# Banded attention and a gated feed-forward block on one core: loads issued as two or four transfers of shorter rows

## The chip, the cores and the metric

The kernel runs on one core of a Trainium2 chip. The metric is the device time of one execution in microseconds (us), taken as the median of several runs. TensorE is called PE here, VectorE DVE, ScalarE ACT, and SyncE SP; SP issues nearly all transfers between the chip's main memory and the on-chip buffer.

## The reference

For 8 batches, 8 heads, 576 positions and 64 numbers per head, queries and keys give scores, and only a band of them is kept: the last 32 positions in heads 0 to 3, every fourth of the last 128 positions in heads 4 to 7. After a softmax the scores weigh the values. The heads of a batch stand side by side as `x`, and a block with a three-tap convolution and a gate follows:

```python
scores = scale * np.matmul(q, k.transpose(0, 1, 3, 2))
scores = np.where(masks[None, :, :, :], scores, -1000000000.0)
...
attn = attn / (np.sum(attn, axis=-1, keepdims=True) + 1e-09)
return np.matmul(attn, v).astype(np.float32)
...
h = np.maximum(x @ w_in, 0.0)            # 512 -> 1024
conv_out += conv_w[k][None, None, :] * hp[:, k:k + S, :]
gate = 1.0 / (1.0 + np.exp(-conv_out))
return (h * gate @ w_out).astype(np.float32)
```

`w_in`, `conv_w` and `w_out` arrive as 64-bit floats, so a weight takes 8 bytes in main memory.

## The kernel before

Attention works on pairs of heads: 8 batches by 4 pairs make 32 units. A unit loads its queries and keys as one tile `qk` of 128 partitions by 1184 numbers (592 KB, rows of 4736 bytes) and its values as one tile `v` of 128 by 768 numbers (384 KB, rows of 3072 bytes). One unit (batch 0, pair 1, by the constant `SPLIT`) has its `qk` load cut in two by columns already, of 608 and 576 numbers, so that PE can begin on the first. There are two `qk` buffers and three `v` buffers; a load into a buffer waits until PE has read what stood there. PE makes the scores in a burst of 72 small matmuls (L281), DVE and ACT make the softmax (L306 to L331), DVE transposes the result (L333), PE multiplies with the values in a burst of 80 or 84 small matmuls (L349), and the result is stored as a high part and a low part, `x…a` and `x…b`.

The feed-forward block of a batch multiplies `x` with `w_in` (L408, results in `mm` or `nn`), makes the convolution and the gate on ACT and DVE (L414 to L432), and multiplies with `w_out` (L448); ACT scales the result (L457) and SP stores it (L463). Each weight is held as a high and a low part too. The function `weights` makes these: it loads a chunk of 1 MB (128 rows of 8192 bytes) into one of two buffers `raw` (L507), and five DVE operations and one ACT copy turn it into the two parts (L513 to L522). There are four such chunks for `w_in` and four for `w_out`.

No loop sets the order of the program. Each piece of work is a task of a planner; the table `TURNS_OF` gives each task its turn, and the tasks are issued in order of their turns. Every engine works through its own instructions in that order. A task that loads a tile is one turn; the table has one entry for each, and its entries are the same before and after the change.

Transfers report through semaphores. The kernel's framework has eight of them for the transfers of SP and ACT (DMAHW0 to DMAHW7 in the rows below) and gives them out in turn, one to each transfer. A transfer that gets a semaphore whose earlier transfer has not landed waits for that landing.

Of the kernel before, what the change touches and what calls it, by code (L numbers as in the profile page):

```python
# [37 lines left out]
I32 = mybir.dt.int32  # L38
# [169 lines left out]
def attn_moe(ctx: ExitStack, tc: tile.TileContext, qk_p, qk_d, v_p, v_d, w_in, w_out, conv, mask, out):  # L208
    nc = tc.nc
# [10 lines left out]
    few = [const.tile([128, 3 * NF], F32, name=f"few{i}") for i in range(2)]  # L220
    plan = Planner()

    def slots(name, n, shape, dtype=F32, parts=1, pool=const):
        make = lambda i: [pool.tile(shape, dtype, name=f"{name}{i}{'abc'[j] if parts > 1 else ''}") for j in range(parts)]
        made = [make(i) for i in range(n)]
        plan.pool(name, made if parts > 1 else [m[0] for m in made])
        return made

    slots("qk", 2, [128, QK])
    slots("v", 3, [128, NV, 128])  # L230
    ss = slots("s", 3, [128, 9, W + 1])
    slots("m", 3, [128, 9])
    slots("z", 3, [128, 9])
# [21 lines left out]
    def attention(b, p):  # L255
        kind = p // 2
        qk, v, s, m, z, pt, x = (Buffer(n) for n in ("qk", "v", "s", "m", "z", "pt", "x"))
# [3 lines left out]
        masked_by_pe = MASKED >> bit & 1  # L261
        xs[b, p] = x
        cuts = (0, S // 2 + 320, QK) if SPLIT >> bit & 1 else (0, QK)
        lqs = [plan.add(lambda lo=lo, hi=hi: nc.sync.dma_start(
            out=qk.t[:, lo:hi], in_=(qk_p, qk_d)[kind][b, p % 2][:, lo:hi]), uses=[qk])
            for i, (lo, hi) in enumerate(zip(cuts, cuts[1:]))]
        lv = plan.add(lambda: nc.sync.dma_start(
            out=v.t, in_=(v_p, v_d)[kind][b, p % 2]), uses=[v])

        block = lambda i: sc[i >= CUT].t[:, W * (i - CUT * (i >= CUT)):][:, 0:W] if early else sc[0].t[:, SC0 + W * i:SC0 + W * i + W]  # L270
        ranges = ((0, CUT), (CUT, 9)) if early else ((0, 9),)
# [2 lines left out]
        def scores(columns, final):  # L274


            for i in range(CUT):
                for c, j, hd, quad, s0, n in TURNS:
                    if i < n and c in columns:
                        q0, k0 = 32 * (s0 + i) + (S // 2 + 608) * c, S // 2 + 32 * (HALVES * c + s0 + i)  # L280
                        nc.tensor.matmul(block(s0 + i)[quad * 32:quad * 32 + 32], qk.t[hd * 64:hd * 64 + 64, q0:q0 + 32],  # L281
                                         qk.t[hd * 64:hd * 64 + 64, k0:k0 + W],
                                         start=not masked_by_pe or (quad, j) not in begun, stop=True,
                                         skip_group_check=True)
                        begun.add((quad, j))
            if masked_by_pe and final:
                for a, z in ((0, CUT), (CUT, 9)):
                    o = sc[a > 0].t[:, 0:W * (z - a)] if early else sc[0].t[:, SC0 + W * a:SC0 + W * z]
                    nc.tensor.matmul(o, ident16, mask_sb[:, kind, W * a:W * z], start=False, stop=True, skip_group_check=True)

        last = None
        for i, lq in enumerate(lqs):
            final = i == len(lqs) - 1
            last = plan.add(lambda cols=(i,) if len(lqs) > 1 else (0, 1), final=final: scores(
                cols, final), [last, lq], [qk, *sc, s])
# [8 lines left out]
        if not masked_by_pe:  # L304
            for a, e in ranges:
                last = plan.add(lambda a=a, e=e: nc.vector.tensor_tensor(  # L306
                    out=s.t[:, a:e, 0:W], in0=span(a, e), in1=masked[:, a:e], op=ALU.add), [last], [*sc, s])
        for a, e in ranges if masked_by_pe else ((0, 9),):
            last = plan.add(lambda a=a, e=e: nc.vector.tensor_reduce(  # L309
                out=m.t[:, a:e], in_=given(a, e), axis=AX.X, op=ALU.max, negate=slotwise), [last], [s, m, *held])  # L310
        if slotwise:
            last = plan.add(lambda: nc.scalar.mul(out=m.t, in_=m.t, mul=SCALE), [last], [m])
# [6 lines left out]
            last = plan.add(exps, [last], [s, m, z, *held])  # L319
            last = plan.add(lambda: nc.scalar.add(out=z.t, in_=z.t, add=1e-9), [last], [z])  # L320
        else:
            for a, e in ranges if masked_by_pe else ((0, 9),):
                last = plan.add(lambda a=a, e=e: nc.vector.tensor_tensor(
                    out=s.t[:, a:e, 0:W], in0=given(a, e), in1=wide(m.t, a, e), op=ALU.subtract), [last], [s, m, *held])
            last = plan.add(lambda: nc.scalar.activation(
                out=flat(), in_=flat(), func=AF.Exp, scale=SCALE), [last], [s])

            last = plan.add(lambda: nc.vector.tensor_reduce(  # L328
                out=z.t, in_=s.t, axis=AX.X, op=ALU.add), [last], [s, z])
        last = plan.add(lambda: nc.vector.reciprocal(out=z.t, in_=z.t), [last], [z])  # L330
        last = plan.add(lambda: nc.vector.tensor_tensor(  # L331
            out=flat(), in0=flat(), in1=wide(z.t), op=ALU.mult), [last], [s, z])
        last = plan.add(lambda: nc.vector.transpose(  # L333
            out=pt.t.rearrange("p (a k) -> p a k", k=W), in_=flat()), [last], [s, pt])
# [20 lines left out]
        last = plan.add(values, [lv, last], [v, pt, tv, x])  # L355

        def made(t):
            whole = tv.t.rearrange("p (c m) -> p c m", c=2)[:, :, TV0:TV0 + 2 * RUN]
            if kind == 0:
                return t.rearrange("p (c m) -> p c m", c=2), whole  # L360
            return t.rearrange("p (m c r) -> p m c r", c=2, r=2), whole.rearrange("p c (r m) -> p m c r", r=2)
# [10 lines left out]
        last = plan.add(lambda: nc.scalar.copy(out=made(x.t[0])[0], in_=made(x.t[0])[1]), [last], [tv, x])  # L372
        if HELPED >> (b * NP + p) & 1:
            def less():
# [3 lines left out]
            last = plan.add(less, [last], [tv, x])  # L378
            return [plan.add(lambda: nc.scalar.copy(
                out=made(x.t[1])[0], in_=made(x.t[1])[1]), [last], [tv, x])]  # L380
# [114 lines left out]
    def weights(src, hi, lo):  # L495

        raw, tb = Buffer("raw"), Buffer("t")
        n = src.shape[1]
        rate = n / PAIRED
        part = lambda i: raw.t[:, 0:2 * n].rearrange("p (n w) -> p n w", w=2)[:, :, i]  # L500
        lw, hw = (lambda i=i: part(i) for i in range(2))
        t = lambda: tb.t[:, 0:n]
        bits = lambda: tb.t.bitcast(I32)[:, 0:n]
        shaped = lambda x, like: x.rearrange("p (a c) -> p a c", a=like.shape[1])
        whole = lambda x: x.rearrange("p a b c -> p a (b c)") if len(x.shape) == 4 else x
        hi, lo = whole(hi), whole(lo)
        load = plan.add(lambda: nc.sync.dma_start(  # L507
            out=raw.t[:, 0:2 * n], in_=src.bitcast(I32)), uses=[raw])

        def step(after, run, uses=(raw, tb)):  # L510
            return plan.add(run, after, uses)

        last = step([load], lambda: nc.vector.tensor_scalar(  # L513
            out=t(), in0=hw().bitcast(F32), scalar1=2.0 ** -112, scalar2=None, op0=ALU.mult))
        last = step([last], lambda: nc.vector.tensor_scalar(  # L515
            out=bits(), in0=bits(), scalar1=3, scalar2=None, op0=ALU.logical_shift_left))
        last = step([last], lambda: nc.vector.scalar_tensor_tensor(  # L517
            out=bits(), in0=hw(), scalar=-0x80000000, in1=bits(), op0=ALU.bitwise_and, op1=ALU.bitwise_or))
        last = step([last], lambda: nc.vector.scalar_tensor_tensor(  # L519
            out=bits(), in0=lw(), scalar=29, in1=bits(), op0=ALU.logical_shift_right, op1=ALU.bitwise_or))  # L520
        high = plan.add(lambda: nc.scalar.copy(out=hi, in_=shaped(t(), hi)), [last], [tb])
        return [high, step([high], lambda: nc.vector.tensor_tensor(  # L522
            out=lo, in0=shaped(t(), lo), in1=hi.bitcast(F32), op=ALU.subtract), [tb])]
# [18 lines left out]
    for h, in hs:  # L542
        nc.gpsimd.memset(h[:, 0:1], 0.0)
        nc.gpsimd.memset(h[:, S + 1:S + 2], 0.0)
    converted = lambda src, pair: weights(src, *pair)
    wired = [converted(w_in[c], (wi[0][c], wi[1][c])) for c in range(4)]
    conved = few_weights(conv)
    wored = [converted(w_out[c], [wo[j][c % 2][:, :, c // 2] for j in range(2)]) for c in range(4)]
    ready = [[attention(b, p) for p in range(NP)] for b in range(B)]
    for b in range(B):  # L550
        expert(b, ready[b], wired, wored, conved)
# [68 lines left out]
```

## Time and profile before

| | |
|---|---|
| median of 3 runs | 511.15 us |
| lowest and highest of them | 510.21 and 513.08 us |
| the profiled execution, its own time | 514.47 us |
| span of the profiled execution, first to last instruction | 512.8 us |
| PE busy with matmuls | 494.7 us, 96% of the span |
| DVE, ACT busy | 370.3 us, 262.2 us |
| bytes moved | 50.95 MB, 99 GB/s over the span |

The span is what the rows of the profile divide up; the time of the execution is 1.67 us longer. The profiled execution is one single execution, 3.3 us above the median of the runs. Idle time of an engine matters only where another engine, or the end, waits for it.

### The profile page before, as it was taken

The page shows a single profiled execution, that of the slowest core. Times are in us where ns is not written, and L with a number is a line of the kernel's source. Part 1 is how long each engine was busy: PE and PEld are TensorE (multiplying, and loading weights), DVE is VectorE, ACT ScalarE, POOL GpSimd, SP SyncE. Part 2 cuts the span into 40 slices and gives each one's busy share as a digit, 9 for nine tenths or more (in the row PEclk, how much of TensorE's full clock was granted, in tenths as well). Part 3 has the DMA queues.
Part 4 walks back from the last instruction along what each step waited for, and adds up shares of the span by engine and source line. Part 5 has one row for each costly group of instructions (what it writes and reads, how often), then busy time and mean ns, then how long its engine had stood idle before and what let it go on. Part 6 is the DMA issues. An engine that isn't in the chain of part 4 may idle for free.

```text
span 512.8 us, 16447 instructions
## 1 busy us (share of the span) xinstructions
PE 494.7 (96%) x7466; PEld 441.0 (86%) x7466; DVE 370.3 (72%) x543; ACT 262.2 (51%) x559; POOL 1.4 (0%) x27
## 2 busy tenths in 40 slices
PE   4797999999999999999999999999999999999997
PEld 2686999999988898888898888889888988999885
DVE  3987999999999888976797558776686227644710
ACT  3547787554654356452664445535464426534611
POOL 1000000000000000000000000000000000000000
PEclk9999899999999999999999999999999999999999
DMA  8957337032432434423133122411120100001111
GB/s 302 366 190 266 111 117 282 1 100 65 140 114 89 146 100 119 141 78 115 32 121 128 62 80 64 129 58 57 32 75 1 42 20 22 22 1 41 42 41 61
DMA packets 16692, 50.95 MB, mean 99 GB/s; under 512 B 2032, under 2 KB 3184, under 8 KB 15600
## 3 DMA queue, kind: packets, MB, share of 16 engines
q1 hardware_dynamic: 16480, 49.84, 29.0%
q8 instruction: 58, 0.95, 0.8%
q10 hardware_dynamic: 144, 0.08, 0.1%
q14 instruction: 10, 0.08, 0.0%
HBM read 40.48 MB, written 9.44 MB: 97 GB/s over the span
## 4 chain that ended last, share of the span: by engine, by line
PE 94%; DVE 3%; DMA 1%; issue 1%; SPq 0%; ACT 0%; ACTq 0%
PE nn L448 40%; PE mm L408 39%; PE att L349 6%; PE att L281 5%; PE nn L408 3%; DMA qk<-in_qk_p_dram 1%; PE att L376 1%; DVE t L517 0%; DVE t L519 0%; DVE m L309 0%; DVE s L331 0%; DVE pt L333 0%; DVE z L328 0%; DVE t L515 0%; DVE t L513 0%
## 5 line engine op out<-in xcount | busy, mean ns | idle before, releaser
L448 PE MATMUL nn<-wo,g 128*128 128x512 f32 (+1 forms) x960 | 227.4, 373 | 0.0
L448 PEld LDWEIGHTS nn<-wo,g 128*128 128x128 f32 x960 | 160.4, 188 | 23.0
L418 DVE SCALAR_TENSOR_TENSOR c<-h,conv_sb,c 128x576 f32<-128x576 f32 x128 | 102.3, 810 | 33.0 <-ACT c L423 32.0
L414 ACT ACTIVATE h<-mm 128x288 f32<-128x288 f32 x120 | 48.6, 409 | 93.5 <-PE mm L408 93.3
L432 DVE TENSOR_TENSOR g<-c,g 128x576 fp32r<-128x576 f32 x64 | 47.8, 751 | 32.9 <-ACT g L431 32.5
L429 DVE SCALAR_TENSOR_TENSOR c<-c,h 128x576 f32<-128x576 f32 x64 | 47.6, 751 | 14.2 <-ACT c L427 13.9
L431 ACT CAST g<-c 128x576 fp32r<-128x576 f32 x64 | 42.5, 671 | 29.4 <-PE nn L448 14.9
L423 ACT ACTIVATE c<-h,conv_sb 128x576 f32<-128x576 f32 x64 | 49.2, 775 | 15.6 <-DVE g L432 15.0
L427 ACT ACTIVATE c<-c 128x576 f32<-128x576 f32 x64 | 42.9, 682 | 20.2 <-DVE c L418 20.0
L457 ACT ACTIVATE out<-nn 128x512 f32<-128x512 f32 (+1 forms) x40 | 21.9, 552 | 47.9 <-PE nn L448 41.8
L408 PE MATMUL mm<-x4a,wi 128*128 128x288 f32 x160 | 45.2, 301 | 0.0
L349 PEld LDWEIGHTS att<-pt,v 32*64 32x64 f32 x2624 | 33.7, 142 | 9.5 <-issue 5.9
L408 PE MATMUL mm<-x2a,wi 128*128 128x288 f32 x144 | 41.2, 301 | 0.0
L408 PE MATMUL mm<-x3a,wi 128*128 128x288 f32 x144 | 40.8, 302 | 0.0
L408 PE MATMUL mm<-x0a,wi 128*128 128x288 f32 x144 | 40.7, 300 | 0.0
L349 PE MATMUL att<-pt,v 32*64 32x64 f32 (+1 forms) x2624 | 37.4, 243 | 2.1 <-DVE pt L333 1.2
L408 PE MATMUL mm<-x6a,wi 128*128 128x288 f32 x128 | 35.7, 300 | 0.0
L408 PE MATMUL mm<-x5a,wi 128*128 128x288 f32 x128 | 35.7, 296 | 0.0
L281 PEld LDWEIGHTS att<-qk 64*32 64x32 f32 x2088 | 23.8, 106 | 11.7 <-issue 7.9
L281 PE MATMUL att<-qk 64*32 64x64 f32 x2088 | 29.0, 227 | 4.9 <-issue 3.2
L408 PE MATMUL mm<-x1a,wi 128*128 128x288 f32 x112 | 32.0, 303 | 0.0
L408 PEld LDWEIGHTS mm<-x4a,wi 128*128 128x128 f32 x160 | 29.8, 188 | 1.5 <-ACT h L414 0.2
(129 smaller groups left out, 748.3 us busy)
## 6 DMA issues: line engine op xcount, KB each, us to landing
qk<-in_qk_d_dram SPq DMA_DIRECT2D x16, 592.0 KB, 4.6
qk<-in_qk_p_dram SPq DMA_DIRECT2D x15, 592.0 KB, 4.3
out_dram<-out SPq DMA_DIRECT2D x28, 256.0 KB, 2.1
v<-in_v_p_dram SPq DMA_DIRECT2D x16, 384.0 KB, 4.4
v<-in_v_d_dram SPq DMA_DIRECT2D x16, 384.0 KB, 3.8
raw<-in_w_in_dram SPq DMA_DIRECT2D x4, 1024.0 KB, 7.0
raw<-in_w_out_dram SPq DMA_DIRECT2D x4, 1024.0 KB, 7.3
out_dram<-out SPq DMA_DIRECT2D x16, 128.0 KB, 2.4
```

The costliest lines, as they stand in the source:

```text
L281: nc.tensor.matmul(block(s0 + i)[quad * 32:quad * 32 + 32], qk.t[hd * 64:hd * 64 + 64, q0:q0 + 32], qk.t[hd * 64:hd * 64 + 64, k0:k0 + W], ...
L349: nc.tensor.matmul(tv.t[hd * 64:hd * 64 + 64, o:o + hi - lo], v.t[quad * 32:quad * 32 + 32, i, hd * 64:hd * 64 + 64], pt.t[quad * 32:quad ...
L408: nc.tensor.matmul(ps.t[:, 0:HALF], wi[jw][fc // 2][:, fc % 2, k], x[k].t[jx][:, hf * HALF:hf * HALF + HALF], start=(k == 0 and i == 0), s ...
L414: relu.append(plan.add(lambda fc=fc, hf=hf, ps=ps: nc.scalar.activation(out=h[fc].t[:, 1 + hf * HALF:1 + hf * HALF + HALF], in_=ps.t[:, 0: ...
L418: nc.vector.scalar_tensor_tensor(out=c[fc].t, in0=h[fc].t[:, k:S + k], scalar=conv_sb[:, k, fc:fc + 1], in1=c[fc].t, op0=ALU.mult, op1=ALU ...
L423: t = plan.add(lambda fc=fc: nc.scalar.activation(out=c[fc].t, in_=h[fc].t[:, 1:S + 1], func=AF.Copy, scale=conv_sb[:, 1, fc:fc + 1]), [re ...
L427: t = plan.add(lambda fc=fc: nc.scalar.activation(out=c[fc].t, in_=c[fc].t, func=AF.Tanh, scale=0.5), [t], [c[fc]])
L429: t = plan.add(lambda fc=fc: nc.vector.scalar_tensor_tensor(out=c[fc].t, in0=c[fc].t, scalar=1.0, in1=h[fc].t[:, 1:S + 1], op0=ALU.add, op ...
L431: hi = plan.add(lambda fc=fc: nc.scalar.copy(out=half(fc, 0), in_=c[fc].t), [t, *(done[fc] if odd else [])], [c[fc], g[fc // 2]])
L432: lo = plan.add(lambda fc=fc: nc.vector.tensor_tensor(out=half(fc, 1), in0=c[fc].t, in1=half(fc, 0).bitcast(F32), op=ALU.subtract), [hi], ...
L448: nc.tensor.matmul(ps.t[:, 0:n], g[k // 2].t[:, k % 2, jg, c0:c0 + 128], w.rearrange("p h c -> p (h c)") if hf is None else w[:, hf], star ...
L457: last = plan.add(lambda ps=ps, o=o, n=n: nc.scalar.mul(out=o.t[:, 0:n], in_=ps.t[:, 0:n], mul=0.5), [last], [ps, o])
```

## The change

A new helper `load` issues a load as several transfers over equal ranges of columns. Loads of `qk` and `v` are issued as two transfers (the `qk` load that was cut in two already becomes four), and each chunk of weights as four. A task still issues all transfers of its load in its one turn, so the table of turns is untouched.

```diff
+    def load(out, src, parts):
+
+        n = out.shape[1]
+        for lo, hi in zip(range(0, n, n // parts), range(n // parts, n + 1, n // parts)):
+            nc.sync.dma_start(out=out[:, lo:hi], in_=src[:, lo:hi])
...
-        lqs = [plan.add(lambda lo=lo, hi=hi: nc.sync.dma_start(
-            out=qk.t[:, lo:hi], in_=(qk_p, qk_d)[kind][b, p % 2][:, lo:hi]), uses=[qk])
+        lqs = [plan.add(lambda lo=lo, hi=hi: load(
+            qk.t[:, lo:hi], (qk_p, qk_d)[kind][b, p % 2][:, lo:hi], 3 - len(cuts) // 2), uses=[qk])
             for i, (lo, hi) in enumerate(zip(cuts, cuts[1:]))]
-        lv = plan.add(lambda: nc.sync.dma_start(
-            out=v.t, in_=(v_p, v_d)[kind][b, p % 2]), uses=[v])
+        lv = plan.add(lambda: load(
+            v.t, (v_p, v_d)[kind][b, p % 2], 2), uses=[v])
...
-        load = plan.add(lambda: nc.sync.dma_start(
-            out=raw.t[:, 0:2 * n], in_=src.bitcast(I32)), uses=[raw])
+        words = plan.add(lambda: load(raw.t[:, 0:2 * n], src.bitcast(I32), 4), uses=[raw])
```

`len(cuts)` is 2 or 3, so the number of parts is 2 in both cases. Rows become 2368 bytes for `qk` (1216 and 1152 where it was cut), 1536 for `v`, and 2048 for weights. The 73 transfers of these loads (33 of `qk`, 32 of `v`, 8 of weights) become 162 (66, 64 and 32).

On SP, at the start of the program, the transfers stood like this before (a row gives the line, the tile written and the tensor read, the shape, and in brackets what the instruction waits for; PE and DVE stand there for their engines' semaphores):

```order
L264 DMA qk_80<-in_qk_p_dram 128x608
L264 DMA qk_80<-in_qk_p_dram 128x576
L480 DMA few_raw<-in_conv_dram 128x48
L264 DMA qk_81<-in_qk_p_dram 128x1184
L507 DMA raw_128<-in_w_in_dram 128x2048
L264 DMA qk_80<-in_qk_d_dram 128x1184 [waits DMAHW2_49,DMAHW1_49,PE_49]
L267 DMA v_82<-in_v_p_dram 128x768
L507 DMA raw_129<-in_w_in_dram 128x2048 [waits DMAHW0_49]
```

In the changed program the same place of SP reads:

```order
L227 DMA qk_80<-in_qk_p_dram 128x304 x2
L227 DMA qk_80<-in_qk_p_dram 128x288 x2
L486 DMA few_raw<-in_conv_dram 128x48
L227 DMA qk_81<-in_qk_p_dram 128x592 x2
L227 DMA raw_128<-in_w_in_dram 128x512 [waits DMAHW0_49]
L227 DMA raw_128<-in_w_in_dram 128x512 [waits DMAHW1_49]
L227 DMA raw_128<-in_w_in_dram 128x512 [waits DMAHW2_49]
L227 DMA raw_128<-in_w_in_dram 128x512 [waits DMAHW3_49]
L227 DMA qk_80<-in_qk_d_dram 128x592 [waits DMAHW4_49,PE_49]
L227 DMA qk_80<-in_qk_d_dram 128x592 [waits DMAHW5_49,PE_49]
L227 DMA v_82<-in_v_p_dram 128x384 [waits DMAHW6_49]
L227 DMA v_82<-in_v_p_dram 128x384 [waits DMAHW7_49]
```

The order of the loads is the same, but the first weight chunk (`raw_128`) now waits, part by part, for the landing of the mask (DMAHW0, issued by ACT) and of the first three parts of `qk_80`, where before it waited for nothing.

On PE, the second unit's scores (reading `qk_81`) and the first unit's product with the values (reading `v_82`) stood like this before:

```order
L281 MATMUL att_131<-qk_81 32x64 [waits DMAHW4_49]
L281 MATMUL att_131<-qk_81 32x64 x35
...
L349 MATMUL att_131<-pt_94,v_82 64x32 [waits DVE_49,DMAHW7_49,Activation_49,Pool_49]
L349 MATMUL att_131<-pt_94,v_82 64x32 x5
L349 MATMUL att_131<-pt_94,v_82 64x64 x28
L349 MATMUL att_131<-pt_94,v_82 64x32 x8
```

and stand like this in the changed program:

```order
L287 MATMUL att_131<-qk_81 32x64 [waits DMAHW6_49]
L287 MATMUL att_131<-qk_81 32x64
L287 MATMUL att_131<-qk_81 32x64 [waits DMAHW7_49]
L287 MATMUL att_131<-qk_81 32x64 x33
...
L355 MATMUL att_131<-pt_94,v_82 64x32 [waits DVE_49,DMAHW6_49,Activation_49,Pool_49]
L355 MATMUL att_131<-pt_94,v_82 64x32 x5
L355 MATMUL att_131<-pt_94,v_82 64x64 x16
L355 MATMUL att_131<-pt_94,v_82 64x64 [waits DMAHW7_49]
L355 MATMUL att_131<-pt_94,v_82 64x64 x11
L355 MATMUL att_131<-pt_94,v_82 64x32 x8
```

A burst now waits for the second part of its tile inside the burst. Counted over the whole program, PE's instructions wait for a transfer's semaphore in 110 places, before in 62.

## Rows read from the trace of the kernel before

**Rows 1.** The page: span, busy time, and PE's busy tenths in 40 slices.
```profile
span 512.8 us, 16447 instructions
PE 494.7 (96%) x7466; PEld 441.0 (86%) x7466; DVE 370.3 (72%) x543; ACT 262.2 (51%) x559; POOL 1.4 (0%) x27
PE   4797999999999999999999999999999999999997
```
**Rows 2.** Chain that ended last, first 64 us: start, us, what.
```profile
2.11 6.17 DMA qk<-in_qk_p_dram
...
10.30 0.76 DVE m L309
...
11.98 0.55 DVE t L513
...
26.71 0.79 DVE pt L333
...
48.31 3.21 issue
51.52 0.44 PE att L281 x26
```
**Rows 3.** SP's timeline at the start: start, us, line, transfer.
```profile
0.74 0.86 SPq L264 DMA_DIRECT2D qk<-in_qk_p_dram  x2
1.64 0.43 SPq L480 DMA_DIRECT2D few_raw<-in_conv_dram  x1
2.11 0.43 SPq L264 DMA_DIRECT2D qk<-in_qk_p_dram  x1
2.59 0.43 SPq L507 DMA_DIRECT2D raw<-in_w_in_dram  x1
```
**Rows 4.** Transfers issued at 2.59, 2.11, 1.64, 0.74, 1.18, 110.99, 75.56; last: us to landing.
```profile
raw<-in_w_in_dram SPq DMA_DIRECT2D x1, 1024.0 KB, 8.2
qk<-in_qk_p_dram SPq DMA_DIRECT2D x1, 592.0 KB, 6.2
few_raw<-in_conv_dram SPq DMA_DIRECT2D x1, 24.0 KB, 3.3
...
qk<-in_qk_p_dram SPq DMA_DIRECT2D x1, 304.0 KB, 3.2
...
qk<-in_qk_p_dram SPq DMA_DIRECT2D x1, 288.0 KB, 3.6
...
qk<-in_qk_p_dram SPq DMA_DIRECT2D x1, 592.0 KB, 3.7
...
qk<-in_qk_p_dram SPq DMA_DIRECT2D x1, 592.0 KB, 4.2
```
**Rows 5.** Busy time by stretch; last columns PE clock, DMA share, GB/s.
```profile
2.00:4.00 2.00, 0.00 (x0) 0.00 (x0) 0.00 (x0) 0.45 (x1) 0.00 (x0) 1.00 0.98 310
4.00:6.00 2.00, 1.98 (x72) 1.84 (x72) 0.94 (x4) 1.44 (x5) 0.00 (x0) 1.00 0.95 227
6.00:8.00 2.00, 0.70 (x4) 0.13 (x2) 1.48 (x4) 0.00 (x0) 0.00 (x0) 1.00 0.98 388
...
10.00:12.00 2.00, 0.27 (x2) 0.00 (x0) 1.70 (x5) 0.87 (x6) 0.00 (x0) 1.00 1.05 429
...
52.50:56.00 3.50, 3.50 (x94) 3.16 (x93) 3.46 (x7) 2.21 (x6) 0.00 (x0) 0.51 0.05 17
```
**Rows 6.** Packets of instructions: whole span, and 49 to 50 us.
```profile
q8 instruction: 58, 0.95, 0.8%
...
q8 instruction: 1, 0.02, 5.8%
```
**Rows 7.** PE timeline, two bursts; the page's group of L408.
```profile
43.92 1.18 PE L281 MATMUL att<-qk 64*32 64x64 f32 x72
...
80.32 0.97 PE L281 MATMUL att<-qk 64*32 64x64 f32 x72
...
L408 PE MATMUL mm<-x4a,wi 128*128 128x288 f32 x160 | 45.2, 301 | 0.0
```

More of the change, by code (lines that the diff above doesn't have):

```diff
@@ L506, in weights @@
         hi, lo = whole(hi), whole(lo)
-        load = plan.add(lambda: nc.sync.dma_start(
-            out=raw.t[:, 0:2 * n], in_=src.bitcast(I32)), uses=[raw])
+        words = plan.add(lambda: load(raw.t[:, 0:2 * n], src.bitcast(I32), 4), uses=[raw])
         def step(after, run, uses=(raw, tb)):
             return plan.add(run, after, uses)
-        last = step([load], lambda: nc.vector.tensor_scalar(
+        last = step([words], lambda: nc.vector.tensor_scalar(
             out=t(), in0=hw().bitcast(F32), scalar1=2.0 ** -112, scalar2=None, op0=ALU.mult))
```

## The prediction

> **What bounds the kernel now.** I read the page first. PE is busy 494.7 of 512.8 us, and of its 40 slices only the first two and the fourth are below nine tenths (the last, at seven, is the end) [rows 1]. So the kernel is PE's work plus the time in which PE stands, 18 us, nearly all of it in the first 52 us. A change to the loads can gain or lose only there, unless it makes a load late that is early now.
>
> The chain of waits says where PE stands. From 2.11 us it goes through one transfer, the second unit's queries and keys, issued at 2.11 and landing 6.17 us later, at 8.28 us. From 10.30 to 27.50 it stays on DVE without a break (first piece `m` L309, last piece `pt` L333), and then it is PE's own work [rows 2]. So in the first 27 us DVE sets the pace, and DVE starts on its chain when the scores of that second load are there. A microsecond saved on this landing is a microsecond saved at 27.5, as long as nothing else on DVE's way is late. The next that could be is the first weight chunk: DVE's L513 needs it at about 11.9 [rows 2]; it was issued at 2.59 and landed 8.2 us later, at 10.8 [rows 3, 4].
>
> The second piece is "issue", 3.21 us at 48.31. It lies inside one burst of 72 score matmuls, of which 26 come after it [rows 2]; the tile had landed, since the first 46 had run. The page means by "issue" that the engine waited for nothing the profile shows. I read it as PE out of instructions: there is a transfer queue named "instruction", 58 packets and 0.95 MB in all (16 KB each), and one packet of it moved between 49 and 50 us, while PE stood [rows 6]. [...] Stall and slow clock together are 4.9 us of the profiled execution.
>
> **The start.** Transfers issued one behind the other are about 0.46 us apart (0.74, 1.64 after two, 2.11, 2.59) [rows 3], of which each takes SP 0.43. Three more of them now stand ahead of the last part of the second load (two of the first unit, one of its own): it is issued at about 2.11 + 3 × 0.46 = 3.5. What speaks for an earlier landing all the same is what follows it. Before, 1 MB of weights was issued 0.48 us behind; now its first part waits for the mask's landing, and the mask is a transfer from the very start. From 2 to 8 us the engines moved 310, 227 and 388 GB/s [rows 5], 1.85 MB, although only 80 (the mask, 128 rows of 320 16-bit numbers) + 304 + 288 + 24 + 592 KB [rows 4] = 1.32 MB had been issued up to the end of the second load; the other half megabyte was weights, moved by engines that had finished their share of the load while others had not. Without it, at the same rates, 1.32 MB are through at 4 + 2 + (1.32 - 0.62 - 0.45) / 0.39 = 6.6 us. From the side of one transfer: 592 KB issued nearly alone lands after 3.7 us [rows 4], half of it should need no more, so 3.5 + 3.7 = 7.2. I take 7.2, a gain of 1.1 us on the chain. The bounds: 6.3 (the rate of 388 all through from 4 us, plus what lies between last packet and landing), a gain of 2.0; and 8.8, a loss of 0.5, if the last part needs 5.3 us from its issue, which is between the 3.7 of a lone load and the 6.2 of the crowded one. The weights must keep up: they are complete at 2.37 MB moved, by these rates at 6 + (2.37 - 1.07) / 0.39 = 9.3, landing by 10; DVE, 1.1 us earlier, needs them at 10.8. The first unit's scores wait for parts issued 0.44 and 0.9 us later than before; DVE's work on them had no hurry, since the chain does not pass through it.
>
> **The instruction packets.** A packet of instructions goes through the same transfer engines as the data. If it waits for a number of rows ahead of it, rows of 1536 to 2368 bytes in place of 3072 to 8192 make that wait half as long or less; at 43 to 45 us two loads of values, a weight chunk and a `qk` load are in flight. The packet moved some time in 49 to 50; asked for at the earliest in the burst at 43.92 [rows 7], it waited up to 5 us. I take 4.5; half of that, 2.2, comes off the stall and leaves 1.0, and I take the clock's 1.7 as gained too, since PE stood for 1.7 us of 10 to 12 at a clock of 1.00 [rows 5]. Bounds: nothing gained, and all 4.9.
>
> [...]
>
> **PE's added waits.** In 48 places more than before PE waits for a transfer, inside the bursts. Most of these transfers landed long before. From below: nothing; the 160 matmuls of L408 on `x4a`, among them many with waits, show 0.0 idle before them [rows 7]. From above: a burst that was broken once took 1.18 us where others take 0.97 [rows 7], 0.2 each, 9.6 in all. A wait for a semaphore that is at its count already is nearest to the rows of L408; I take one lost turn of the burst's pace each, 0.97 / 72 = 13 ns, 0.6 us in all.
>
> **What is hidden.** 89 more transfers cost SP about 0.4 us each, 36 us over the run. The tightest load behind the start is the `qk` load of 75.56, landing 4.2 us later [rows 4] at 79.8, for a burst at 80.32 [rows 7]. Its second part goes 0.4 us later but carries half; if it lost all of 0.4 the margin of 0.5 would still cover it. Without that cover every tenth shows on PE. Stores stand behind one or three more issues on SP; PE waits for a store through two output buffers only, and the chain has no store in it.
>
> **Sum.** For the profiled execution: 514.47 - 1.1 - 2.2 - 1.7 + 0.6 = 510.1 us. It lies 3.3 us above the median of the runs. Without stall and slow clock it would be 509.6, so the median execution, 511.15, has at most about 1.6 us of them if all else is equal; I take the same share as gained, 3.9 / 4.9, so 1.3. For the median: 511.15 - 1.1 - 1.3 + 0.6 = 509.4. I predict **509.6**, between the two.
>
> **Rivals.** *Both gains in full*: the timed runs have the stall as the profiled one has, and lie lower for another reason: 511.15 - 1.1 - 3.9 + 0.6 = 506.8. For it speaks that the runs spread by 2.9 us, as a stall that comes and goes would make them; against it, the 3.3 us to the profiled one. Chance 0.20. *Nothing comes of it*: the second load, issued 1.4 us later in its last part, lands when it did, and the packet of instructions waits for bytes, not for rows: 511.15 + 0.6 = 511.7. Chance 0.25.
>
> *Slower by the fixed cost of a transfer*: even 24 KB took 3.3 us to land [rows 4]. If the four parts of the first weight chunk, held back by the waits for landings, pay it one after the other, the chunk lands at about 4.8 (the first unit's second half: 1.18 + 3.6) + 4 × 3.3 = 18 us in place of 10.8, and DVE's chain stands from 11.9: + 6.1 - 1.3 + 0.6, so 516.5. It makes the kernel slower by over 0.5% from a landing at about 15 on. Against it: transfers issued at 0.74 and 1.18 landed after 3.2 and 3.6 us [rows 4], 0.8 us apart for 288 KB, so the fixed parts overlap. Chance 0.06. [...]
>
> *Slower by PE's waits*: 0.2 us at each of 48 places gives 511.15 - 1.1 - 1.3 + 9.6 = 518.4; it decides from about 0.1 each. The break of the burst at 43.92 speaks for it, the L408 rows against it. Chance 0.05.
>
> **How the numbers follow.** The forecast has 0.44. About 0.5% (2.6 us) is what a measurement can tell here: faster means under 508.6, slower over 513.7. A quarter of the forecast (more of the stall than I think in the timed runs) and the first rival are faster: 0.11 + 0.20 = 0.31. The two slower rivals make 0.10 after rounding, the rest 0.59. The range leaves out those two and the outer edges of the first two rivals: 506.5 to 512.3; the forecast's own range is 508 to 511.
>
> **What would show it.** The second `qk` load landing near 7.2 instead of 8.28, DVE's chain starting near 9.2, `pt` before the values at about 26.4; no piece "issue" over 1.5 us near 48, and a clock of 1.00 from 50 to 60; bursts of 72 still at 0.97 to 1.0 us. I am wrong if the second load lands after 8.3, if the first weight chunk lands after DVE is ready for it, or if a stall of the same kind stands elsewhere.

## The result: 0.5% slower, and the profile after

The changed kernel takes 512.85 us (median of 20 runs, 511.20 to 519.91). The kernel before takes 510.42 us in 20 runs beside it (507.32 to 513.08); the 511.15 I reckoned from was the median of three. The ratio is 1.0052, with a 95% interval of 1.0030 to 1.0073: slower, by 2.4 us between the medians and 2.7 (1.5 to 3.7) by the ratio. Three executions far above the others of their kernels (519.91 us here, 542.22 and 923.98 in two experiments) are in no ratio. The forecast of 509.6 was wrong, in sign and size, and the time lies outside its range.

The two profiled executions tell the opposite. The one after took 511.92 us, 0.9 below the median of its kernel; the one before took 514.47, 4.0 above its own. So [rows 1 to 7] are those of an execution well above its median, and a row of after that looks better need not be the change's doing. The page after:

```profile
span 510.1 us, 16579 instructions
PE 494.2 (97%) x7466; PEld 439.5 (86%) x7466; DVE 370.6 (73%) x543; ACT 262.1 (51%) x559; POOL 1.4 (0%) x27
PE   4799999999999999999999999999999999999997
...
q1 hardware_dynamic: 29296, 49.85, 30.4%
q8 instruction: 58, 0.95, 0.8%
```

It answers to [rows 1]: PE is as busy as before, and its idle time is at the start still. The same bytes go in 29296 packets of data (q1), 16480 before. The chain of waits up to 64 us (start, us, what), which answers to [rows 2]:

```profile
3.54 4.96 DMA qk<-in_qk_p_dram
...
10.47 0.76 DVE m L315
...
12.12 0.70 DVE t L518
...
36.23 0.72 PE att L287 x49
37.48 0.48 PE nn L414 x3
37.96 6.25 DMA qk<-in_qk_d_dram
44.25 0.89 PE att L287 x55
...
52.65 0.95 issue
```

The second load's last part lands at 3.54 + 4.96 = 8.50 us, where I had said 7.2, and `m` starts at 10.47, where I had said 9.2. The piece "issue" of 3.21 us at 48.31 is gone; one of 0.95 stands at 52.65. And there is a piece that stood nowhere before: a `qk` load issued at 37.96 that lands at 44.21, with PE waiting for it.

SP's timeline at the start, which answers to [rows 3]:

```profile
0.74 1.81 SPq L227 DMA_DIRECT2D qk<-in_qk_p_dram  x4
2.60 0.43 SPq L486 DMA_DIRECT2D few_raw<-in_conv_dram  x1
3.07 0.91 SPq L227 DMA_DIRECT2D qk<-in_qk_p_dram  x2
4.03 1.86 SPq L227 DMA_DIRECT2D raw<-in_w_in_dram  x4
```

The issues stand where the prediction put them (last part of the second load at 3.54). But the weights did not stay away: their first part was issued at 4.03, 0.49 us behind, for the mask that it waits for had landed (issued at 0.74, 2.8 us to landing). The stretches (us, then busy time of PE, PEld, DVE, ACT, POOL, PE's clock, the transfer engines' share, GB/s) answer to [rows 5]:

```profile
2.00:4.00 2.00, 0.02 (x4) 0.05 (x5) 0.41 (x1) 0.86 (x2) 0.00 (x0) 1.00 0.94 230
4.00:6.00 2.00, 1.69 (x53) 1.47 (x57) 0.29 (x3) 0.59 (x4) 0.00 (x0) 1.00 1.06 316
6.00:8.00 2.00, 1.79 (x35) 0.92 (x26) 0.98 (x4) 0.45 (x3) 0.00 (x0) 1.00 0.90 280
...
52.50:56.00 3.50, 2.55 (x21) 2.40 (x20) 3.50 (x6) 3.33 (x20) 0.00 (x0) 1.00 0.80 267
```

From 2 to 8 us 1.65 MB were moved (230, 316 and 280 GB/s for 2 us each), before 1.85, with the engines about as busy. From 52.5 to 56 the clock is 1.00, where it was 0.51.

### The profile page after: what moved, and what is told of

Same layout as the page of the kernel before. It is cut to its first block, busy times and chain, and to the rows that moved or that the text cites. A ratio compares the mean times of both kernels' runs of the same rounds, so it can differ in the third digit from the quotient of the medians.

```text
span 510.1 us, 16579 instructions
## 1 busy us (share of the span) xinstructions
PE 494.2 (97%) x7466; PEld 439.5 (86%) x7466; DVE 370.6 (73%) x543; ACT 262.1 (51%) x559; POOL 1.4 (0%) x27
## 3 DMA queue, kind: packets, MB, share of 16 engines
q1 hardware_dynamic: 29296, 49.85, 30.4%
## 4 chain that ended last, share of the span: by engine, by line
PE 95%; DMA 2%; DVE 1%; issue 1%; ACT 0%; SPq 0%; DVEq 0%; ACTq 0%
PE nn L454 40%; PE mm L414 39%; PE att L355 7%; PE att L287 5%; PE nn L414 3%; DMA qk<-in_qk_d_dram 1%; PE att L382 1%; DMA qk<-in_qk_p_dram 1%; SPq L227 0%; PE mm L287 0%; DVE m L315 0%; DVE pt L339 0%; DVE t L518 0%; DVE z L334 0%; DVE s L337 0%
## 5 line engine op out<-in xcount | busy, mean ns | idle before, releaser
L287 PEld LDWEIGHTS att<-qk 64*32 64x32 f32 x2088 | 24.1, 106 | 9.2 <-issue 5.0
L287 PE MATMUL att<-qk 64*32 64x64 f32 x2088 | 29.7, 227 | 1.9 <-DMA qk<-in_qk_d_dram 0.8
```

## The experiments

Each ratio is to runs of the kernel before on the same chip, with its 95% interval. Where the edit is a count of loads, the helper counts its calls in the order of issue, and `parts` is 1 for the others. Where it counts, lines stand 3 further down (L290 for L287).

### One kind of load at a time

**The kernel before once more.** No edit.

> The kernel before, unchanged, for a second profile. Theory 1 (the profiled execution of before was an odd one: its stall of 3.21 us at 48 us and the 3.4 us of lower clock after it are not in most executions): no piece called issue over 1 us near 48 us, span about 508 to 509. Theory 2 (the stall belongs to the kernel, and the changed kernel lost time elsewhere): the stall of about 3 us is there again, span about 512.

One execution, 510.12 us, span 508.4. PE's waits for instructions from 15 to 110 us (what ended the wait: us, times, longest):

```profile
PE mm L408 <- issue: 1.5, 1, 1.5
PE att L281 <- issue: 0.8, 1, 0.8
...
PE nn L408 <- issue: 0.3, 1, 0.3
```

The stall of 3.21 us at 48 [rows 2] was one execution's. Here the kernel before has three shorter ones, 2.6 us in all, and none over 1.5. And `m` behind the second load starts at another time, 8.93 instead of 10.30:

```profile
8.93 0.76 DVE L309 TENSOR_REDUCE m<-att 128x9 f32<-128x576 f32 x1 [1.09 <-PE att L289]
```

**Only `qk`, only `v`, only the weights.** The other kinds get one part:

```diff
-            qk.t[:, lo:hi], (qk_p, qk_d)[kind][b, p % 2][:, lo:hi], 3 - len(cuts) // 2), uses=[qk])
+            qk.t[:, lo:hi], (qk_p, qk_d)[kind][b, p % 2][:, lo:hi], 1), uses=[qk])
...
-            v.t, (v_p, v_d)[kind][b, p % 2], 2), uses=[v])
+            v.t, (v_p, v_d)[kind][b, p % 2], 1), uses=[v])
...
-        words = plan.add(lambda: load(raw.t[:, 0:2 * n], src.bitcast(I32), 4), uses=[raw])
+        words = plan.add(lambda: load(raw.t[:, 0:2 * n], src.bitcast(I32), 1), uses=[raw])
```

> Only the loads of queries and keys are issued in halves; values and weight chunks whole. Theory A (the loss is at the start and comes from the last part of the second load being issued later): the whole loss is here, ratio about 1.004. Theory B (it comes from the weights in four parts, held back by waits for landings): 1.000. Theory C (PE's waits inside bursts, over the whole run): half of it, 1.002, and matmul 7465 drifts against matmul 2000 by about 1 us.

> Only the loads of values are issued in halves. Theory A: 1.000, since no load of values stands ahead of the second load of queries and keys. Theory B: 1.000. Theory C: 1.002.

> Only the weight chunks are issued in four parts. Theory A: 1.000, or faster, since the second load is issued as early as before and the weights behind it no longer run ahead. Theory B: the whole loss, 1.005. Theory C: 1.000.

Only `qk`: 1.0017 (0.9991 to 1.0042). Only `v`: 1.0010 (0.9985 to 1.0035). Only the weights: 1.0043 (1.0012 to 1.0074). The middle values are nearest to theory B, but the three intervals overlap, and the trace speaks against B's way: with the weights in parts the first chunk's four parts, issued from 2.58 to 4.07, land after 6.5 us (median), none later than 10.8 us, when the whole chunk landed in the kernel before. `m` starts at 10.60 with `qk` in parts, at 9.67 and 9.69 in the two others:

```profile
10.60 0.76 DVE L315 TENSOR_REDUCE m<-att 128x9 f32<-128x576 f32 x1 [1.83 <-PE att L295]
```

With the weights in parts, PE waits 1.0 us for a load of values between 30 and 60 us:

```profile
PE att L355 <- DMA v<-in_v_p_dram: 1.0, 1, 1.0
```

### The first loads, the later ones, rows in place of columns

```diff
+    calls = []
...
+        calls.append(out)
+        parts = parts if len(calls) <= 16 else 1
```

> Only the first 16 loads are split, those that were issued in the first 34 us of the profile after (three of `qk`, then weights, queries, values up to the fourth weight chunk); the other 57 are whole as before. Theory A (the loss is made in the crowded start: the second load's last part is issued later, and shorter rows take more time of transfer engines that are busy without a break): this kernel has the whole loss, 1.004 to 1.006 of the kernel before, the last landing of the first 16 loads lies near 33.5 us as after the full change, not near 31 as before, and behind 60 us nothing differs. Rival B (PE's added waits inside bursts and SP's added issues over the whole run cost it): of 162 transfers it has 89 fewer added ones left than the full change but for 23 or so, so about a quarter of the loss, 1.001 to 1.002.

> The other way round: the first 16 loads are whole, the 57 later ones split. Theory A: 0.999 to 1.001 of the kernel before, with the second load landing where it lands when it is whole (6.9 to 8.3 us). Rival B: 1.003 to 1.005, with matmul time from 60 us to the end longer by 1.5 to 2.5 us.

The first 16 loads: 1.0031 (1.0007 to 1.0054), the later 57 (`> 16` in place of `<= 16`): 1.0028 (1.0005 to 1.0051). Theory A was wrong on the second, and theory B has its size but not its way: from the piece `nn` x39 of the chain to its last, `nn` x120, this kernel takes 367.49 us (109.30 to 476.79), the kernel before 367.12 and, in its second trace, 367.04, a difference of 0.4 where B wanted 1.5 or more (from 60 us on). The trace has PE waiting, between 30 and 60 us, for the `qk` load that stands in the changed kernel's chain too, and never in the two traces of the kernel before:

```profile
PE att L290 <- DMA qk<-in_qk_d_dram: 0.8, 2, 0.4
```

**As many transfers, by rows.** The helper cuts the 128 partitions and leaves the columns whole:

```diff
-        n = out.shape[1]
+        n = 128
...
-            nc.sync.dma_start(out=out[:, lo:hi], in_=src[:, lo:hi])
+            nc.sync.dma_start(out=out[lo:hi], in_=src[lo:hi])
```

> Every load is split into as many transfers as in the change, in the same order, but by rows: two transfers of 64 rows in place of two of half the columns, four of 32 rows for weights. So the rows stay at 4736, 3072 and 8192 bytes, and the number of packets is that of the kernel before. Theory A1 (shorter rows cost, by their packets): the first 16 loads have landed near 31 us again, and what is left is the later issue of the second load, 0.5 to 1 us: 1.001 to 1.002. Theory A2 (the number of transfers costs, by SP's 0.47 us for each ahead of the second load and by the waits for their semaphores, whatever their rows): 1.004 to 1.006 as with the change.

1.0496 (1.0470 to 1.0523), 24.7 us slower. Neither theory had this, and it does not tell them apart, for the cut by rows has a cost of its own. From 2 to 12 us and from 12 to 30 us:

```profile
2.00:12.00 10.00, 5.85 (x148) 3.77 (x148) 3.04 (x9) 2.65 (x7) 0.00 (x0) 1.00 0.95 226
12.00:30.00 18.00, 7.28 (x280) 5.97 (x282) 13.83 (x23) 5.78 (x24) 0.00 (x0) 1.00 1.03 232
```

The same two stretches of the kernel before:

```profile
2.00:12.00 10.00, 4.61 (x148) 3.21 (x148) 4.19 (x13) 3.45 (x13) 0.00 (x0) 1.00 0.98 348
12.00:30.00 18.00, 14.27 (x417) 12.09 (x418) 17.86 (x30) 11.08 (x44) 0.00 (x0) 1.00 0.94 357
```

The transfer engines are as busy (shares of 0.95 and 1.03, in the kernel before 0.98 and 0.94) and move a third less (226 and 232 GB/s in place of 348 and 357). Why they do, no run here shows.

**One transfer fewer ahead of the second load.** In the kernel before, ACT issues the 24 KB of `few_raw`:

```diff
-        last = plan.add(lambda: nc.sync.dma_start(
-            out=few_raw, in_=src.bitcast(I32).rearrange("p (n t) -> p n t", t=2)))
+        last = plan.add(lambda: None)
...
     nc.scalar.dma_start(out=kinds_sb, in_=mask)
+    nc.scalar.dma_start(out=few_raw, in_=conv.bitcast(I32).rearrange("p (n t) -> p n t", t=2))
```

> The kernel before, with one edit: the 24 KB of convolution weights, which SP issues ahead of the second load, are issued by ACT instead, right behind the mask. So the second load is issued at about 1.64 instead of 2.11 us. If the second load's landing sets the start, as I hold, it lands about 0.4 us earlier, DVE's first `m` starts 0.4 us earlier, and the time is 0.999 of the kernel before (at the limit of what five rounds show; the profile shows it by DVE's start, 9.3 or less against 8.9 to 10.3 in kernels with a whole second load). Rival: the transfer engines are busy from 2 us on with whatever was issued, the second load lands where it did, and nothing changes, 1.000.

1.0015 (0.9997 to 1.0033), no gain. The load was issued at 1.64 us, and took longer: it landed at 1.64 + 6.11 = 7.75, and `m` started at 9.76, as with whole loads issued at 2.11. The rival held.

```profile
1.64 6.11 DMA qk<-in_qk_p_dram
9.76 0.76 DVE m L309
```

### The start alone, and the dose doubled

> Only the first three loads are split (the two of the first unit's queries and keys, and the second unit's); the other 70 are whole. Theory C (the second load lands later since its last part is issued 1.4 us later, and DVE's chain with it): DVE's first `m` after the second load starts at 10.3 to 10.9 as in the kernels with split `qk` loads (whole: 8.9 to 9.8), and the time is 1.0015 to 1.002 of the kernel before. Rival D (the loss in the first wave comes from the shorter rows of the weights and values that follow): `m` starts where it starts with whole loads, time 1.000.

The first three loads alone (`len(calls) <= 3`): 1.0025 (1.0000 to 1.0050), `m` at 10.35. Theory C holds against D.

Then the kernel before, with three transfers of 1 KB ahead of its second load, into a tile that nothing reads:

```diff
+        def fetch(lo, hi):
+            if (b, p) == (0, 0):
+                for i in range(3):
+                    nc.sync.dma_start(out=extra[:, i], in_=conv.bitcast(I32)[:, 0:2])
+            nc.sync.dma_start(out=qk.t[:, lo:hi], in_=(qk_p, qk_d)[kind][b, p % 2][:, lo:hi])
...
```

> The kernel before with all its loads whole, and three added transfers of 1 KB each (two words for each partition, into a tile that nothing reads) just ahead of the second load, so that it is issued 1.4 us later, as its last part is in the change, with rows as long as before. Theory C1 (the place in SP's order costs): `m` starts 0.7 to 1.4 us later than in the kernel before, at 10.2 to 11, and the time is 1.0015 to 1.0025. Theory C2 (the shorter rows of the load cost): no later start, 1.000.

1.0036 (1.0017 to 1.0055), with all rows long. But `m` started at 9.97, ahead of the 10.2 to 11 forecast, in an execution that also had a stall of 1.6 us at 64. The load was issued at 3.53 and landed at 7.96:

```profile
3.53 4.43 DMA qk<-in_qk_p_dram
```

Whole loads issued at 2.11 land from 6.92 to 8.29 in seven traces, the split one from 8.38 to 8.88 in six. So the three transfers ahead make the kernel slower, but this trace does not show that they do it by a late landing: as in the run before, the place in SP's order moved the landing little. What makes up the 1.0036 stays open.

> The dose doubled: `qk` loads as four transfers, weight chunks as eight, values as three; 292 transfers for the 73 loads, 219 added in place of 89. If the loss comes from transfers and packets added (theory A for the start, B for the run), it grows with them: 1.010 to 1.013, with the second load's `m` start near 11.5 to 12.5 us and, if PE's waits inside bursts have a share, matmul time behind 105 us longer by 1 us than before (398.98 to 400). If the 1.005 of the change comes from a chance shift of where PE runs out of instructions, it does not grow: 1.003 to 1.007.

```diff
+        parts = {2: 4 if len(out.shape) == 2 else 3, 1: 2, 4: 8}[parts]
```

1.0226 (1.0196 to 1.0256), well above the forecast, and no chance shift. `m` starts at 11.99. From 2 to 12 us only 219 GB/s are moved at a share of 0.84, which fits SP's pace (parts of 72 to 148 KB, one each 0.47 us at best), and the loads fall behind PE. Its longest wait:

```profile
PE att L290 <- DMA qk<-in_qk_d_dram: 5.1, 2, 4.8
```

These 5.1 us stand at the same `qk` load for the burst that begins near 43 us in the change (here it was due at 46): the place that breaks first when SP is late.

> The first 16 loads whole, the 57 later ones as four, three and eight transfers. The 1.0028 (1.0005 to 1.0051) that the later loads alone had was against theory A, which expects nothing. If it is real and a cost of added transfers or waits, it grows to 1.004 to 1.007 here, and the trace shows where, behind 34 us. If it was chance, or no more than PE's waits in bursts (0.4 us of 510): 1.001 to 1.002.

1.0038 (1.0011 to 1.0066), against 1.0028 for the single dose. The trace has 1.3 us of waits for that `qk` load. From `nn` x39 to `nn` x120 it takes 366.95 us (113.42 to 480.37): behind 110 us even this dose costs nothing.

### Which places: a table of two by two, and the last two runs

> The changed kernel, but the fifth weight chunk (the first of `w_out`, issued near 34.5 us, ahead of the `qk` load for the burst near 43.5) is one transfer; the other 72 loads are split as in the change. Theory E (the four issues of this chunk, 2.6 us in all, push its bytes into the time of the `qk` load behind it, which then lands after PE is ready): the chunk's landing comes nearer to its issue, the `qk` load lands before the burst begins, PE's two waits of 0.4 us are gone, and the time is 0.8 us less than the changed kernel's in the same batch, about 1.0035 of the kernel before. Rival F (the split of the `qk` load itself makes it late): the two waits stay, 1.005.

> The changed kernel, but the first three loads (the first unit's and the second unit's queries and keys) are whole. If the later start is its own term of about 0.9 us: `m` starts near 9.4 instead of 10.5, PE's two waits near 43 stay, and the time is 1.003 to 1.0035 of the kernel before. Rival (weights and values that follow in short rows set the pace of the first 30 us, so an earlier start of DVE is given back before 27 us): 1.005.

> The changed kernel with both edits: the first three loads and the fifth weight chunk whole, 69 of 73 loads split. If the two places are the whole loss: 0.999 to 1.002, with no wait of PE on a load near 43 and `m` at 9.3 to 9.7. If a cost is spread over all loads (packets, SP's issues, PE's waits), most of the loss stays: 1.003 to 1.005.

> The changed kernel as it is, on the same chip as the three others: 1.004 to 1.006 again, `m` start at 10.3 to 10.7, PE waiting twice near 43 us for the `qk` load, 0.3 to 0.5 each. If the two waits are missing here, they were chance.

The edits are `len(calls) != 17`, `len(calls) > 3`, both, and none. The ratios: one chunk whole 1.0042 (1.0017 to 1.0067), first three whole 1.0035 (1.0011 to 1.0059), both 1.0030 (1.0006 to 1.0054), the change again 1.0030 (1.0010 to 1.0049). The intervals overlap, and the table does not settle it by times: both whole gives the 1.0030 of the change itself, which the expectation had for a cost spread over all loads. Averaged over the single executions of the table, those with the first three split are 0.7 us longer than those with them whole (95% interval -0.1 to 1.6), and those with the chunk split 0.1 shorter (-1.0 to 0.8). The traces give two things. `m` starts at 10.64 and 10.80 where the first three are split, at 9.54 and 9.87 where they are whole. And the change again has no wait near 43; its burst runs in 0.97 us, although one of its waits for a transfer stands inside it:

```profile
44.49 0.97 PE L287 MATMUL att<-qk 64*32 64x64 f32 x72
```

PE came to it at 44.49, in the first trace of the change at 43.14; the load's last part had been issued at 39.29 and landed 4.3 us later, at 43.6. So that wait comes in some executions only, and its absence with one chunk whole proves nothing.

```diff
+        parts = parts if parts == 4 and len(calls) > 16 else 1
...
+        parts = parts if len(calls) > 3 and not (parts == 4 and len(calls) > 16) else 1
```

> The kernel before, with only the four chunks of `w_out` (the 5th to the 8th weight chunk) split in four; 69 of 73 loads whole. If these chunks carry what is left (their parts hold SP for 1.9 us and more, and move bytes into the time of the loads behind them): 1.002 to 1.003. If they do not: 0.999 to 1.001.

> The changed kernel with the first three loads and the four chunks of `w_out` whole; 66 of 73 loads split. If the first three loads and the `w_out` chunks are the whole loss: 0.999 to 1.001. If the cost is spread over all loads: 1.002 to 1.003.

Only the four chunks of `w_out`: 1.0006 (0.9978 to 1.0034), nothing to be told, though PE's waits have a load that is whole here and yet late:

```profile
PE att L290 <- DMA qk<-in_qk_d_dram: 0.8, 1, 0.8
```

All but those four and the first three: 0.9998 (0.9976 to 1.0020). 66 of 73 loads are in parts, and no loss is left that the run can tell. PE's waits for instructions from 15 to 110 us are these, and it waits for no load from 30 us on:

```profile
PE mm L417 <- issue: 1.7, 1, 1.7
...
PE att L290 <- issue: 0.3, 1, 0.3
```

## Why the prediction was wrong, step by step

**The start was the step that failed first.** I gave the second load a landing at 7.2 us and a gain of 1.1. That DVE's chain hangs on this landing, and PE on that chain, was right: from `m` to the `pt` that ends the chain it takes 16.4 us in the profile before (10.30 to 26.71) and 16.5 after (10.47 to 27.01), and PE's product burst behind this `pt` (27.55 before, 27.96 after) starts 17.2 to 17.9 us behind `m` in all 18 traces (the doubled dose of all loads and the cut by rows left out). The landing was wrong. I let the engines move the second load at their rate of 388 GB/s, with the weights held back. They were not held back (4.03), and the rate was not kept: from 2 to 4 us 230 GB/s were moved in place of 310, from 6 to 8 us 280 in place of 388, with busy shares of 0.94 and 0.90 against 0.98 twice. The last part took 4.96 us from its issue, where I had given it 3.7. Whether SP's pace does this (parts of 144 and 152 KB, one each 0.47 us, are at most 0.32 MB per us), or the shorter rows at engines that are busy, no run tells apart; the later issue by itself does not show in the landing (7.96 for the whole load issued at 3.53). I also measured against a late start: `m` at 10.30 in the profile of before. Six traces with the first three loads split as in the change have `m` at 10.35 to 10.85, mean 10.62 (the change twice, `qk` alone, the first wave, the first three, one chunk whole). Ten with them whole and no other edit ahead of them have 8.93 to 10.30, mean 9.71 (before twice, `v` alone, weights alone, the two kernels with only later loads split, first three whole, both, the last two). So the term is a loss of 0.9 us, 2.0 from the forecast; the first three alone measure 1.0025, or 1.3 us (0 to 2.6). The loss reaches PE at 28 us (the product burst starts at 28.0 on average in the six traces, at 27.2 in the ten). By `nn` x39 it is lost in the spread of the executions (109.30 to 114.47; means 111.5 and 111.2).

**The gain from the instruction packets is not shown.** I took 1.3 us of the median as gained. The 3.21 us and the slow clock belonged to one execution. That this clock (0.51 granted from 52.5 to 56) cost 1.7 of the 4.9 us, no run shows: the same 93 matmuls, six of L408, the product burst of 84 and three more, take 3.71 us there (52.40 to 56.11) and 2.44 us in the profile after at a clock of 1.00 (49.38 to 51.82), 1.3 us less. From 15 to 110 us PE waits for instructions 1.9 and 1.2 us in the two traces of the change, 3.2 and 2.6 in the two of the kernel before, which would fit. But over all traces the two kinds overlap: 1.2 to 2.8 us in the six with 66 loads or more in parts (mean 2.1, with the same two left out), 1.7 to 4.5 in the seven with 8 or fewer (mean 2.8). A gain of 0.7 us is possible; no run shows it. The clock gave nothing either: in the second series the mean granted clock was 0.993 in the changed kernel's executions and 0.998 in those of the kernel before, and the times do not go with it (the shortest of the changed kernel's, 510.88 us, had 0.98). That the wait goes with the rows was a supposition of mine, neither borne out nor refuted by these totals; no run here measures one packet's wait. I had named a rival by which the packet waits for bytes and not for rows; that stays open too.

**What I called hidden was not.** I took the load of 75.56 as the tightest. The one for the burst at 43 us is tighter where the chunk of `w_out` ahead of it is in four: SP then takes 2.58 us over the chunk in place of 0.33, and its bytes fall into the `qk` load's time (its last part, issued at 36.63, lands 5.1 us later, at 41.7, where the whole chunk landed at 34.18 + 5.8 = 40.0). SP's timeline after:

```profile
34.48 2.58 SPq L227 DMA_DIRECT2D raw<-in_w_out_dram  x4
37.53 3.39 SPq L227 DMA_DIRECT2D qk<-in_qk_d_dram  x4
```

and of before:

```profile
34.18 0.33 SPq L507 DMA_DIRECT2D raw<-in_w_out_dram  x1
38.43 2.96 SPq L264 DMA_DIRECT2D qk<-in_qk_d_dram  x2
```

The `qk` load leaves about as early before its burst as it did (37.53 for 43.14, before 38.43 for 43.92), its parts take 6.1 us to land (median) where the whole took 4.1, and the burst breaks twice:

```profile
43.55 0.30 PE L287 MATMUL att<-qk 64*32 64x64 f32 x4 [0.41 <-DMA qk<-in_qk_d_dram]
44.25 0.89 PE L287 MATMUL att<-qk 64*32 64x64 f32 x68 [0.40 <-DMA qk<-in_qk_d_dram]
```

Of seven traces with that chunk in four or eight parts (the same two left out) five show a wait of 0.8 us or more for a load between 30 and 60 us; of eleven with it whole none shows more than 0.2. The split of the `qk` load is not needed for it: in the run with only the chunks of `w_out` split it was whole and late all the same. That the spread of SP's issues is the way is argued from the two timelines, not shown apart; and the times of the table above show no gain from the chunk whole.

**PE's added waits: the size was near, the price per wait was not.** I gave 0.6 us, the same for each wait. From `nn` x39 to `nn` x120 the change takes 367.44 and 367.38 us, the kernel before 367.12 and 367.04: 0.3 us. The rival of 0.2 us a place falls. But the waits do not cost alike. All eight traces with the later values in halves take 367.35 to 367.68 us, nine of the ten others 366.72 to 367.17 (the tenth, with three transfers ahead, falls behind evenly over the whole stretch, to 367.96). Only `qk` in halves takes 366.78, and the later loads in four, three and eight parts, with more waits, 366.95. So the cost goes with the values cut in two: the 23 product bursts behind 110 us take 25.35 to 25.62 us with that cut and 24.91 to 25.17 without. Why just that cut costs, no run tells.

**The rivals.** *Slower by the fixed cost* had its time near the result (516.5; measured 512.85), but not its way: the first weight chunk's parts were issued 0.47 us apart, landed after 5.1 to 5.7 us each and by 11.2, and DVE's `t` at L518 starts 1.65 us behind `m`, as it did (1.68). *Nothing comes of it* (511.7) was nearest; it lacked the later start.

**The sum.** In place of -1.1 - 1.3 + 0.6 the traces give +0.9 (start), 0 to -0.7 (packets), +0.3 (PE's waits), and 0.8 or nothing (the burst at 43; 0.4 on average over the change's two traces): 0.9 to 1.6 us. Measured by the ratios are 2.7 (1.5 to 3.7) and, in the second series, 1.5 (0.5 to 2.5). So the sum reaches the lower edge of the first at best, and a part of the loss has no place yet. One reading of [rows 1] was off besides: of the 18 us in which PE stands, 3.7 are the end behind its last matmul (509.1 of 512.8), not the start; no term hung on it. Open is why both places undone still gave 1.0030 while the three other chunks of `w_out` whole besides gave 0.9998: those chunks may cost as the first does, but alone they measure 1.0006, and the intervals of all three overlap.

No version here beats the kernel before.

## What to carry to other kernels

Splitting a load moved everything behind it on SP, by 0.47 us a part, and at the start, with the transfer engines busy (0.90 to 1.06 from 2 to 8 us in the profile after), the second load's last part landed later than the whole did (8.65 us on average for 7.8). Look for the loads that an engine waits for, at the start and behind each large transfer, and leave those whole; elsewhere 66 of 73 loads could be split with no cost and no gain that the run could tell (0.9976 to 1.0020). Before a stall in a profile is counted as something to be gained, see it in a second execution, for the one profiled was 4 us from its median here. And take the margin of each load from its landing and its burst, not from one load that looks tight.

## What the runs showed of the hardware beside that

From 2 to 12 us the kernel with transfers to 64 and 32 partitions moved 226 GB/s at a busy share of 0.95, the kernel before 348 GB/s at 0.98. And some of the spread between executions of one kernel is made near 30 us: the two traces of the kernel before are 0.9 us apart at the product burst (27.55 and 26.68) and 2.5 at the next score burst (37.30 and 34.80). The same four matmuls, 128 by 288 into `mm` from `x1a` (lowest, middle and highest ns, from and to us), stand like this in the kernel before, in the change again, and in the kernel with the first three loads split:

```profile
L408 PE MATMUL mm<-x1a,wi x4: 442/442/442, 29.8 to 33.0; 128*128 128x288 f32 x4
```
```profile
L414 PE MATMUL mm<-x1a,wi x4: 442/442/442, 30.5 to 33.7; 128*128 128x288 f32 x4
```
```profile
L417 PE MATMUL mm<-x1a,wi x4: 295/296/297, 29.6 to 31.5; 128*128 128x288 f32 x4
```

The granted clock reads 1.00 for 28 to 36 us in all three, and the second trace of the kernel before has both durations (294 to 442). This goes with the execution and not with the change; what sets it was not tried.
